# q loads cut by head, early loads gated behind weights, and v of batch 0 put ahead of the weights, in an attention and token/channel mixer kernel

## The chip, the cores and the metric

One core of a Trainium2 chip runs the whole program. The metric is device time in microseconds (us) of one launch; lower is better. The change is compared with the kernel before on the same inputs.

## What is computed

For 8 batches, 8 heads, 576 positions and head width 64, attention in which a position sees its neighbours within 32, and 8 global positions see and are seen by all; then a token mixer and a channel mixer on the 576 x 512 result.

```python
mask = (abs(pos[:, None] - pos[None, :]) <= 32) | is_global[:, None] | is_global[None, :]
attn = softmax(where(mask, q @ k.T / 8, -1e9))
x = attn @ v                                   # heads side by side: 576 x 512
u = x + (relu(x.T @ w_tok1) @ w_tok2).T        # w_tok1 576 x 256
out = u + relu(u @ w_ch1) @ w_ch2              # w_ch1 512 x 1536
```

Inputs and output are float32; the kernel computes in float16 with float32 sums.

## The kernel before, in words

Each engine runs its instructions in the order in which the program text issues them; nothing is reordered, so the text is the schedule. A batch goes through these stages: q and k are loaded as float32, cast to float16 (q on ACT, `cast_q`; k on POOL, `cast_k`), and transposed in 32 x 32 blocks on DVE (`Xk`, `Xq`). v is loaded in five pieces of 128 (the outer ones 96) rows, `load_v`, L94, and cast on POOL or ACT (`vcast`, L193). `S_step` makes the banded scores on PE and their exponentials on ACT (L259 to L265), `S_mask` multiplies by the band on DVE (L276), `GK` handles the global queries, `OG` (L304) the rows of the global positions, `PV` (L324 to L337) the product with v. `M1` to `M3` are the token mixer and a transpose, and `M4` (L411, weights wc1) and `M5` (L437, weights wc2) are the channel mixer, called dense here. `M4` and `M5` of batch b are merged, step by step, with the attention stages of batches b+1 and b+2. `fill(n)` issues n matmuls on zeros in the start.

The start (L560 to L717) is written out by hand for batch 0, and nothing dense lies beside it. SP issues all loads of q, v and later k, and all stores; POOL issues the loads that cast to float16 on the way (k of batch 0, w1, w2, wc1, wc2) and gathers q and k of the global positions (gq, gk). For batch 0, SP issues q for the two groups of four heads (hg = 0, 1), then v; POOL's weights stand ahead of its casts of v (L664 to L672, then L690). `load_qk(1)` and `load_v(1)` follow on SP. Later `load_wc2` stands on POOL ahead of the casts of v of batch 1 (L759, and `VC(1)` at L769).

Two points of order matter below. ACT casts both halves of q of batch 0 (L642) ahead of the first exponential, and all four casts of q of batch 1 (L136) ahead of the first ReLU of dense 0 (L414). And the builder gives SP's transfers eight completion semaphores in turn (DMAHW0 to DMAHW7 in the rows of the order; DMASW0 to 7 for POOL's): a transfer waits until the one eight before it has landed.

The load of q of one head group names the four heads as the outermost dimension of its source:

```python
nc.sync.dma_start(out=d[:, hg, 0 : 16 * D], in_=src[:, 0 : 4 * P].rearrange("h (i r) d -> h i (r d)", r=16))
```

Of the kernel before, what the change touches and what calls it, by code (L numbers as in the profile page):

```python
# [17 lines left out]
P = 128  # L18
# [13 lines left out]
def kernel(  # L32
# [79 lines left out]
    def load_q(b, hg):  # L112
        d = st[b]["q32"]
        src = q[b, 4 * hg : 4 * hg + 4]
        nc.sync.dma_start(out=d[:, hg, 0 : 16 * D], in_=src[:, 0 : 4 * P].rearrange("h (i r) d -> h i (r d)", r=16))
        nc.sync.dma_start(out=d[:, hg, 16 * D :], in_=src[:, 4 * P : S].rearrange("h (i r) d -> h i (r d)", r=2))

    def alloc_32(b):
# [4 lines left out]

    def load_qk(b):
        alloc_32(b)
        if b == 1:
            nc.gpsimd.memset(st[b]["k32"][:, :, RK * D - 2 : RK * D], 0.0)
        for hg in range(2):
            nc.sync.dma_start(
                out=st[b]["k32"][:, hg], in_=k[b, 4 * hg : 4 * hg + 4].rearrange("h (i r) d -> (h i) (r d)", i=32)  # L130
            )
            load_q(b, hg)
# [528 lines left out]

    nc.gpsimd.memset(n32v[0][0:WIN, 0], 0.0)
    nc.gpsimd.memset(n32v[0][P - WIN : P, NT - 1], 0.0)
    nc.gpsimd.dma_start(out=w1, in_=moe_w_tok1[0 : S - LAST, :].rearrange("(c p) x -> p c x", p=P))  # L664
    nc.gpsimd.dma_start(out=w1l[0:LAST, 0], in_=moe_w_tok1[S - LAST : S, :])
    nc.gpsimd.dma_start(out=w2[:, :, 0:S], in_=moe_w_tok2.rearrange("(c p) x -> p c x", p=P))

    def eg_const(i):
        for g in range(2):
            nc.gpsimd.tensor_copy(out=egs[i][:, :, :, g, NG:16], in_=ohk.unsqueeze(2).to_broadcast([P, NT, 4, NG]))  # L670

    load_wc1()  # L672
    eg_const(0)
    fill(FILL[1])
    u_S(0, 0, 0)()
    fill(FILL[2])
# [10 lines left out]
    )  # L687
    nc.vector.tensor_scalar(out=mf[:, 4 * QS :], in0=it_f[:, 4 * P : S], scalar1=gpp, scalar2=hi8, op0=ALU.is_equal, op1=ALU.max)
    globals_k(0, nc.vector)
    vcast(0, (0, 1, 2))  # L690
    load_qk(1)
    load_v(1)
    nc.gpsimd.memset(n32v[1][0:WIN, 0], 0.0)
    nc.gpsimd.memset(n32v[1][P - WIN : P, NT - 1], 0.0)
    make_identity(nc, ident)
# [2 lines left out]
    eg_const(1)  # L698
    globals_(1, nc.gpsimd)
    globals_k(1)  # L700
    u_S(0, 1, 1)()
    vcast(0, (3, 4), nc.scalar)
    fill(FILL[8])
# [51 lines left out]
    for hg in range(2):  # L755
        for half in range(2):
            cast_k(1, hg, half)
            cast_q(1, hg, half)
    load_wc2()  # L759
    nc.gpsimd.dma_start(out=w1l[LAST:P, 1], in_=moe_w_tok1[S - LAST : S, :])  # L760
    load_qk(2)
    load_v(2)
    for _, f in X_units(1):
        f()

    for b in range(B):
        D4, D5 = dense(b)
        if b == 0:
            merge(gap(2.5) + VC(1) + phase_s(1), D4)  # L769
            merge(gap(2.0) + weave(phase_og(1) + M1u(1), C(2)) + weave(phase_m(1), G(2) + X_units(2)), D5)  # L770
            flush()
            gather(gq, q, 1)
            gather(gk, k, 1)
        elif b == 1:
            merge(VC(2) + phase_s(2) + gap(1.0) + weave(phase_og(2) + M1u(2), C(3)), D4)
            for _, f in G(3) + X_units(3):
                f()
            gather_t(gq, gqT, 1)
            gather_t(gk, gkT, 1)
            merge(VC(3) + weave(mix(phase_m(2), phase_s(3))[:-2], C(4)) + mix(phase_m(2), phase_s(3))[-2:], D5)  # L780
            flush()
        else:
            A, Bs = [], []
            if b + 1 < B:
                A += phase_og(b + 1) + M1u(b + 1)
                Bs += phase_m(b + 1)
            if b + 2 < B:
                A = G(b + 2) + weave(A, X_units(b + 2) + VC(b + 2))
                Bs = mix(Bs, phase_s(b + 2))
            if b + 3 < B:  # L790
                Bs = weave(Bs[:-2], C(b + 3)) + Bs[-2:]
            merge(A, D4)
            merge(Bs, D5)
            flush()
# [30 lines left out]
```

## Time and profile before

| | |
|---|---|
| median of 3 runs | 369.27 us (368.64 to 370.51) |
| the profiled execution: its own time | 365.77 us |
| its span, first to last instruction | 364.1 us |
| mean granted TensorE clock | 0.958 |
| PE busy | 322.1 us (88%) |
| DVE, ACT, POOL busy | 188.8, 161.2, 74.5 us |
| data moved by DMA | 41.55 MB, mean 114 GB/s |

Times in the rows are microseconds from the start of the span. PE is the matrix engine, DVE the vector engine, ACT the activation engine, POOL the general engine, SP the engine that issues most transfers; SPq marks such an issue. A row of the timeline gives start, duration, engine, line, operation, out<-in with shapes, how many were merged (x), and in brackets how long the engine had stood idle and what released it. In a table of windows, the DMA share is the mean busy share of the core's 16 DMA engines: 0.25 is four of sixteen all the time. Transfers of several queues overlap on an engine, so it can be above 1. Bytes are counted where they land, so a float32 weight that is cast on the way counts half.

### The profile page before, as it was taken

What the parts mean: (1) busy time and instruction counts of PE and PEld (TensorE: products, weight loads), DVE (VectorE), ACT (ScalarE), POOL (GpSimd) and SP (SyncE); (2) the same over time, 40 slices, a digit from 0 to 9 for tenths busy, and PEclk for the clock granted to TensorE, in tenths of its full rate; (3) what the DMA queues carried; (4) which work ended last, traced back from release to release, by engine and by line L of the source; (5) the groups of instructions that cost most, each with busy time, mean ns of one, the idle gap of its engine ahead of it and who ended that gap; (6) DMA issues with size and microseconds to landing.
All of it is one profiled execution on the core that took longest, in us unless ns stands there. A gap on an engine that the chain in (4) does not pass through costs nothing.

```text
span 364.1 us, 7413 instructions
## 1 busy us (share of the span) xinstructions
PE 322.1 (88%) x3092; PEld 164.3 (45%) x3092; DVE 188.8 (52%) x355; ACT 161.2 (44%) x301; POOL 74.5 (20%) x155
## 2 busy tenths in 40 slices
PE   7239698798889996799989999999899999999994
PEld 2113453363436642354445644644466445545541
DVE  6257355464785753682659148745864466244021
ACT  5144128932295454242844546354645254411600
POOL 5711640326206001410141002300330000000000
PEclk9558899999899998999999999999999999999999
DMA  3996549847964937755164514511000021002012
GB/s 77 165 199 126 162 115 200 200 133 150 241 198 128 224 115 182 208 163 127 58 187 153 113 58 134 160 55 59 32 32 0 31 85 35 0 31 86 0 59 87
DMA packets 54738, 41.55 MB, mean 114 GB/s; under 512 B 39984, under 2 KB 46000, under 8 KB 54704
## 3 DMA queue, kind: packets, MB, share of 16 engines
q1 hardware_dynamic: 49136, 36.58, 36.3%
q0 software_dynamic: 5568, 4.49, 8.4%
q8 instruction: 24, 0.39, 0.5%
q14 instruction: 10, 0.08, 0.1%
HBM read 36.12 MB, written 9.44 MB: 125 GB/s over the span
## 4 chain that ended last, share of the span: by engine, by line
PE 53%; DMA 10%; ACT 6%; DVE 5%; SPq 2%; issue 2%; POOL 2%; POOLq 0%; DVEq 0%
PE b1p L411 17%; PE op L437 17%; DMA q<-in_q_dram 9%; DVE e_all L276 4%; PE hp L373 4%; PE a1p L357 3%; PE s L250 3%; PE b1lp L424 2%; ACT e_all L259 2%; PE pv L332 2%; PE pv L324 2%; PE pu L391 1%; PE pv L337 1%; SPq L94 1%; ACT e_all L265 1%
## 5 line engine op out<-in xcount | busy, mean ns | idle before, releaser
L437 PE MATMUL op<-wc,b 128*128 128x512 f16 x384 | 94.9, 380 | 0.0
L411 PE MATMUL b1p<-uT,wc 128*128 128x512 f16 x384 | 92.8, 383 | 0.9 <-ACT b L414 0.9
L414 ACT ACTIVATE b<-b1p 128x512 f16<-128x512 f32 x96 | 57.4, 601 | 65.6 <-PE b1p L411 65.3
L276 DVE TENSOR_TENSOR e_all<-e_all,bandm 128x1000 f16<-128x1000 f16 x64 | 40.1, 687 | 24.9 <-ACT e_all L265 24.8
L437 PEld LDWEIGHTS <-b 128*128 128x128 f16 x384 | 34.8, 98 | 38.8 <-issue 4.2
L411 PEld LDWEIGHTS <-wc 128*128 128x128 f16 x384 | 34.4, 98 | 38.8 <-issue 4.4
L441 DVE TENSOR_TENSOR osb<-u,op 128x512 f32<-128x512 f16 x32 | 22.0, 686 | 40.6 <-PE op L437 33.5
L259 ACT ACTIVATE e_all<-s 128x800 f16<-128x800 f32 x32 | 25.1, 837 | 39.8 <-PE s L250 39.5
L378 DVE TENSOR_TENSOR u<-x,hp 128x1024 f16<-128x1024 f16 x14 | 17.1, 1222 | 42.9 <-PE hp L373 42.9
L250 PE MATMUL s<-qT,kT 32*128 32x200 f16 (+1 forms) x640 | 23.1, 253 | 18.1 <-DVE qT L198 7.9
L279 POOL COPY eg<-e_all 128x160 f16<-128x160 f16 x14 | 5.2, 368 | 146.5 <-DVE e_all L276 146.5
L193 POOL CAST vsh<-v 128x512 f16<-128x512 f32 x38 | 23.4, 644 | 31.9 <-DMA v<-in_v_dram 31.9
L250 PEld LDWEIGHTS <-kT 32*128 32x128 f16 x640 | 13.3, 98 | 34.8 <-issue 27.9
L344 DVE TENSOR_TENSOR x<-pv,rr 128x512 f16<-128x512 f32 (+1 forms) x40 | 27.6, 691 | 1.4
L332 PE MATMUL pv<-vsh,e_all 128*128 128x66 f16 x320 | 28.1, 195 | 0.0
L332 PEld LDWEIGHTS <-e_all 128*128 128x128 f16 x320 | 24.3, 98 | 5.1 <-issue 0.5
L140 POOL CAST k<-k 128x576 f16<-128x576 f32 x28 | 17.8, 665 | 42.3 <-DVE kT L212 17.7
L136 ACT CAST q<-q 128x576 f16<-128x576 f32 x28 | 18.4, 681 | 15.6 <-DMA q<-in_q_dram 15.5
L102 PE MATMUL w<-zz 128*128 128x512 f16 x66 | 23.4, 475 | 1.3 <-DVE p_i L149 1.3
L337 PE MATMUL pv<-vsh,e_all 128*128 128x66 f16 x256 | 23.8, 195 | 0.0
L324 PE MATMUL pv<-rf,lf 128*128 128x264 f16 x80 | 22.0, 279 | 0.0
L212 DVE STREAM_TRANSPOSE kT<-k 128x576 int32<-128x576 int32 x16 | 19.9, 1242 | 3.7 <-DMA k<-in_k_dram 3.6
(134 smaller groups left out, 352.0 us busy)
## 6 DMA issues: line engine op xcount, KB each, us to landing
q<-in_q_dram SPq DMA_DIRECT2D x16, 512.0 KB
out_dram<-osb SPq DMA_DIRECT2D x32, 256.0 KB
k<-in_k_dram SPq DMA_DIRECT2D x14, 576.0 KB
v<-in_v_dram SPq DMA_DIRECT2D x24, 256.0 KB
v<-in_v_dram SPq DMA_DIRECT2D x16, 192.0 KB
wc<-in_moe_w_ch_dram POOLq DMA_DIRECT2D x6, 512.0 KB, 13.8
q<-in_q_dram SPq DMA_DIRECT2D x16, 64.0 KB
out_dram<-osb SPq DMA_DIRECT2D x8, 128.0 KB
```

The source lines that it names most:

```text
L102: nc.tensor.matmul(ps, lhsT=zz[:, 0:P], rhs=zz, start=True, stop=True)
L193: (nc.scalar.copy if eng else nc.gpsimd.tensor_copy)(out=vsh[b % 2][:, c, :, 0:D], in_=n32v[b % 2][:, c])
L250: nc.tensor.matmul(tiles[r // 2][:, r % 2, off : off + n], lhsT=kT[rs, P * c : P * c + P, e], rhs=qf[rs, lo : lo + n, e], start=(e == 0), ...
L259: nc.scalar.activation(out=e2[:, :, 1:3, 64:EW], in_=ps[:, :, 0:400].rearrange("p h (c x) -> p h c x", c=2), func=AF.Exp, scale=scale)
L276: nc.vector.tensor_mul(out=eh, in0=eh, in1=bandm)
L324: nc.tensor.matmul(ps[:, hf, 0 : 4 * VW], lhsT=lfs[b % 2][:, QS * tau - sh : QS * tau - sh + P], rhs=s["rf"][:, 4 * hf : 4 * hf + 4, :], s ...
L332: nc.tensor.matmul(o, lhsT=e_all[:, h, tau, QS - sh : QS - sh + P], rhs=vs[:, tau, h, :], start=False, stop=last and tau == NT - 1,)
L337: nc.tensor.matmul(o, lhsT=e_all[:, h, tau + 1, 0:P], rhs=vs[:, tau + 1, h, :], start=False, stop=last)
L344: nc.vector.tensor_tensor(out=x16[r, tau, :].rearrange("p (f h x) -> p f h x", f=2, h=4), in0=pq[r, :, :, 0:D], in1=rr[r].unsqueeze(3).to_ ...
L411: nc.tensor.matmul(ps, lhsT=wc1[:, cc, P * j : P * j + P], rhs=s["uT"][:, cc, :], start=(cc == 0), stop=(cc == 3))
L414: nc.scalar.activation(out=s["b1"][:, j, :], in_=ps, func=AF.Relu)
L437: nc.tensor.matmul(ps, lhsT=w, rhs=wc2[:, j, :], start=(j == 0), stop=(j == NJ - 1))
```

## The change

Four things. `load_q` issues four transfers of one head each (32 partitions x 1024) in place of one of four heads; the small rest (128 rows of 128) stays as it was. Ahead of the q and k loads of batches 1 and 2 stands a transfer of two float16 elements out of a weight tile into the k buffer: for batch 1 out of the second third of wc1, for batch 2 out of the second third of wc2. It can start only when that third has landed, and the load of k, which overwrites the same place, can start only after it. On POOL the weights of the start are moved behind the casts of v of batch 0 (w1 behind pieces 0 and 1, w2 and wc1 behind piece 2), and wc2 behind the casts of pieces 0 to 2 of v of batch 1; `load_qk(1)` and `load_v(1)` move down in the text. `VC(1)` is dissolved: its casts and `load_v(3)` stand ahead of dense 0.

```diff
--- before.py
+++ after.py
@@ -112,7 +112,11 @@
     def load_q(b, hg):
         d = st[b]["q32"]
         src = q[b, 4 * hg : 4 * hg + 4]
-        nc.sync.dma_start(out=d[:, hg, 0 : 16 * D], in_=src[:, 0 : 4 * P].rearrange("h (i r) d -> h i (r d)", r=16))
+        for r in range(4):
+            nc.sync.dma_start(
+                out=d[32 * r : 32 * r + 32, hg, 0 : 16 * D],
+                in_=src[r, 0 : 4 * P].rearrange("(i r) d -> i (r d)", r=16),
+            )
         nc.sync.dma_start(out=d[:, hg, 16 * D :], in_=src[:, 4 * P : S].rearrange("h (i r) d -> h i (r d)", r=2))
 
     def alloc_32(b):
@@ -123,8 +127,9 @@
 
     def load_qk(b):
         alloc_32(b)
-        if b == 1:
-            nc.gpsimd.memset(st[b]["k32"][:, :, RK * D - 2 : RK * D], 0.0)
+        if b in (1, 2):
+            src = wc1[0:1, 0, 512:514] if b == 1 else wc2[0:1, 4, 0:2]
+            nc.sync.dma_start(out=st[b]["k32"].bitcast(F16)[0:1, 0, 0:2], in_=src)
         for hg in range(2):
             nc.sync.dma_start(
                 out=st[b]["k32"][:, hg], in_=k[b, 4 * hg : 4 * hg + 4].rearrange("h (i r) d -> (h i) (r d)", i=32)
@@ -661,16 +666,18 @@
 
     nc.gpsimd.memset(n32v[0][0:WIN, 0], 0.0)
     nc.gpsimd.memset(n32v[0][P - WIN : P, NT - 1], 0.0)
-    nc.gpsimd.dma_start(out=w1, in_=moe_w_tok1[0 : S - LAST, :].rearrange("(c p) x -> p c x", p=P))
-    nc.gpsimd.dma_start(out=w1l[0:LAST, 0], in_=moe_w_tok1[S - LAST : S, :])
-    nc.gpsimd.dma_start(out=w2[:, :, 0:S], in_=moe_w_tok2.rearrange("(c p) x -> p c x", p=P))
 
     def eg_const(i):
         for g in range(2):
             nc.gpsimd.tensor_copy(out=egs[i][:, :, :, g, NG:16], in_=ohk.unsqueeze(2).to_broadcast([P, NT, 4, NG]))
 
+    eg_const(0)
+    vcast(0, (0, 1))
+    nc.gpsimd.dma_start(out=w1, in_=moe_w_tok1[0 : S - LAST, :].rearrange("(c p) x -> p c x", p=P))
+    nc.gpsimd.dma_start(out=w1l[0:LAST, 0], in_=moe_w_tok1[S - LAST : S, :])
+    vcast(0, (2,))
+    nc.gpsimd.dma_start(out=w2[:, :, 0:S], in_=moe_w_tok2.rearrange("(c p) x -> p c x", p=P))
     load_wc1()
-    eg_const(0)
     fill(FILL[1])
     u_S(0, 0, 0)()
     fill(FILL[2])
@@ -687,9 +694,6 @@
     )
     nc.vector.tensor_scalar(out=mf[:, 4 * QS :], in0=it_f[:, 4 * P : S], scalar1=gpp, scalar2=hi8, op0=ALU.is_equal, op1=ALU.max)
     globals_k(0, nc.vector)
-    vcast(0, (0, 1, 2))
-    load_qk(1)
-    load_v(1)
     nc.gpsimd.memset(n32v[1][0:WIN, 0], 0.0)
     nc.gpsimd.memset(n32v[1][P - WIN : P, NT - 1], 0.0)
     make_identity(nc, ident)
@@ -698,6 +702,8 @@
     eg_const(1)
     globals_(1, nc.gpsimd)
     globals_k(1)
+    load_qk(1)
+    load_v(1)
     u_S(0, 1, 1)()
     vcast(0, (3, 4), nc.scalar)
     fill(FILL[8])
@@ -756,17 +762,20 @@
         for half in range(2):
             cast_k(1, hg, half)
             cast_q(1, hg, half)
+    nc.gpsimd.dma_start(out=w1l[LAST:P, 1], in_=moe_w_tok1[S - LAST : S, :])
+    vcast(1, (0, 1, 2))
     load_wc2()
-    nc.gpsimd.dma_start(out=w1l[LAST:P, 1], in_=moe_w_tok1[S - LAST : S, :])
+    vcast(1, (3, 4))
     load_qk(2)
     load_v(2)
+    load_v(3)
     for _, f in X_units(1):
         f()
 
     for b in range(B):
         D4, D5 = dense(b)
         if b == 0:
-            merge(gap(2.5) + VC(1) + phase_s(1), D4)
+            merge(gap(2.5) + phase_s(1), D4)
             merge(gap(2.0) + weave(phase_og(1) + M1u(1), C(2)) + weave(phase_m(1), G(2) + X_units(2)), D5)
             flush()
             gather(gq, q, 1)
```

SP at the start of the program, before (q_0 and k_1: q of batch 0, k of batch 1):

```order
L84 DMA gidx_i<-in_global_idx_dram 128x16
L115 DMA q_0_118<-in_q_dram 128x1x1024
L116 DMA q_0_118<-in_q_dram 128x1x128
L115 DMA q_0_118<-in_q_dram 128x1x1024
L116 DMA q_0_118<-in_q_dram 128x1x128
L94 DMA v_0_85<-in_v_dram 96x8x64
L94 DMA v_0_85<-in_v_dram 128x8x64 x3
L94 DMA v_0_85<-in_v_dram 96x8x64
L129 DMA k_1_364<-in_k_dram 128x1152
```

And SP there in the changed kernel:

```order
L84 DMA gidx_i<-in_global_idx_dram 128x16
L116 DMA q_0_118<-in_q_dram 32x1024 x4
L120 DMA q_0_118<-in_q_dram 128x1x128
L116 DMA q_0_118<-in_q_dram 32x1024 x4
L120 DMA q_0_118<-in_q_dram 128x1x128
L94 DMA v_0_85<-in_v_dram 96x8x64
L94 DMA v_0_85<-in_v_dram 128x8x64 x3
L94 DMA v_0_85<-in_v_dram 96x8x64
L132 DMA k_1_384<-wc_107 1x2x1
L134 DMA k_1_384<-in_k_dram 128x1152
```

The order of q, v, k is the same; four rows of 32 partitions stand for each row of 128, and the gate (L132) has come ahead of k of batch 1. With the semaphores that each waits for, SP around the gate in the changed kernel reads:

```order
L94 DMA v_0_85<-in_v_dram 96x8x64 [waits DMAHW7_49]
L132 DMA k_1_384<-wc_107 1x2x1 [waits DMAHW0_49,DMASW2_49]
L134 DMA k_1_384<-in_k_dram 128x1152 [waits DMAHW1_49,DMAHW0_49]
L116 DMA q_1_383<-in_q_dram 32x1024 [waits DMAHW2_49,Activation_49]
L116 DMA q_1_383<-in_q_dram 32x1024 [waits DMAHW3_49]
```

DMASW2 is the semaphore of the second third of wc1, DMAHW0 then that of the gate. POOL from the gathers on, before (w_104, w_106: w1, w2; wc_107: wc1; vsh_100: v of batch 0 in float16):

```order
L183 DMA gk<-in_k_dram,idx_i 128x64 x2
L662 MEMSET v_0_85 32x512
L663 MEMSET v_0_85 32x512
L664 DMA w_104<-in_moe_w_tok_dram 128x4x256
L665 DMA w1l<-in_moe_w_tok_dram 64x256
L666 DMA w_106<-in_moe_w_tok_dram 128x2x576
L230 DMA wc_107<-in_moe_w_ch_dram 128x4x512 x3
L670 COPY eg_96<-ohk 128x20x8 x2
L193 CAST vsh_100<-v_0_85 128x8x64 x3
```

And POOL there in the changed kernel:

```order
L188 DMA gk<-in_k_dram,idx_i 128x64 x2
L667 MEMSET v_0_85 32x512
L668 MEMSET v_0_85 32x512
L672 COPY eg_96<-ohk 128x20x8 x2
L198 CAST vsh_100<-v_0_85 128x8x64 x2
L676 DMA w_104<-in_moe_w_tok_dram 128x4x256
L677 DMA w1l<-in_moe_w_tok_dram 64x256
L198 CAST vsh_100<-v_0_85 128x8x64
L679 DMA w_106<-in_moe_w_tok_dram 128x2x576
L235 DMA wc_107<-in_moe_w_ch_dram 128x4x512 x3
```

Each weight is now issued only after a cast that waits for a piece of v. On ACT, DVE and PE no instruction is added, removed or moved.

## Rows read from the trace of the kernel before

**Rows 1.** Table of windows, the start and the rest: us, engines, granted clock, DMA share, GB/s.

```profile
0.00:56.00 56.00, 36.10 (x319) 16.95 (x320) 27.93 (x89) 19.58 (x33) 25.00 (x54) 0.79 0.71 142
56.00:364.00 308.00, 286.05 (x2775) 147.33 (x2773) 160.89 (x267) 141.58 (x269) 49.50 (x101) 0.99 0.40 109
```

**Rows 2.** Timeline of SP, the first 40 us.

```profile
1.28 0.74 SPq L115 DMA_DIRECT2D q<-in_q_dram  x1
...
9.52 25.37 SPq L94 DMA_DIRECT2D v<-in_v_dram  x5
37.39 0.35 SPq L129 DMA_DIRECT2D k<-in_k_dram  x1
```

**Rows 3.** Timeline, all engines, the start: DVE, ACT, PE and POOL's waiting instructions.

```profile
8.56 1.26 DVE L212 STREAM_TRANSPOSE kT<-k 128x576 int32<-128x576 int32 x1 [1.36 <-DMA k<-in_k_dram]
...
13.32 1.15 ACT L642 CAST q<-q 128x1152 f16<-128x1152 f32 x1 [7.75 <-DMA q<-in_q_dram]
...
16.16 0.86 PE L250 MATMUL s<-qT,kT 32*128 32x200 f16 x16 [7.93 <-DVE qT L198]
...
18.48 1.26 DVE L212 STREAM_TRANSPOSE kT<-k 128x576 int32<-128x576 int32 x1 [2.29 <-DMA k<-in_k_dram]
...
22.49 1.15 ACT L642 CAST q<-q 128x1152 f16<-128x1152 f32 x1 [8.01 <-DMA q<-in_q_dram]
23.55 1.56 ACT L259 ACTIVATE e_all<-s 128x800 f16<-128x800 f32 x2
...
24.68 1.16 DVE L650 TENSOR_TENSOR bandm<-band,rowok 128x1000 f16<-128x1000 f16 x1
...
27.78 2.45 DVE L276 TENSOR_TENSOR e_all<-e_all,bandm 128x1000 f16<-128x1000 f16 x4
...
34.70 0.24 DVE L279 COPY eg<-e_all 128x160 f16<-128x160 f16 x1
...
36.70 0.61 POOL L193 CAST vsh<-v 128x512 f16<-128x512 f32 x1 [1.57 <-DMA v<-in_v_dram]
...
37.88 1.33 ACT L193 CAST vsh<-v 128x512 f16<-128x512 f32 x2 [4.72 <-POOL v L693]
...
39.93 0.63 PE L304 MATMUL og<-vsh,eg 128*32 128x132 f16 x20 [3.96 <-ACT lf L295]
...
55.75 2.40 ACT L136 CAST q<-q 128x576 f16<-128x576 f32 x4
...
55.93 1.89 PE L411 MATMUL b1p<-uT,wc 128*128 128x512 f16 x8
```

**Rows 4.** Table of windows of 2 us: columns as in rows 1.

```profile
24.00:26.00 2.00, 1.14 (x24) 0.68 (x23) 1.93 (x4) 1.10 (x2) 0.00 (x0) 0.50 1.22 197
...
122.00:124.00 2.00, 2.00 (x32) 1.74 (x30) 1.30 (x5) 1.85 (x4) 0.00 (x0) 1.00 1.14 288
...
128.00:130.00 2.00, 2.00 (x14) 0.75 (x16) 1.22 (x1) 0.00 (x0) 0.00 (x0) 1.00 0.25 100
```

**Rows 5.** Timeline of SP from 90 us: five pieces of v with little beside them.

```profile
89.76 5.71 SPq L94 DMA_DIRECT2D v<-in_v_dram  x5
```

**Rows 6.** The page's DMA issues: wc1 and wc2, KB landed each, us to landing.

```profile
wc<-in_moe_w_ch_dram POOLq DMA_DIRECT2D x6, 512.0 KB, 13.8
```

**Rows 7.** Table of windows 87:91, 93:99, 101:105, 138:142 and 148:152, its sum.

```profile
sum 22.00, PE 12.09 PEld 5.63 DVE 14.30 ACT 9.69 POOL 5.42; mean PE 2.42 PEld 1.13 DVE 2.86 ACT 1.94 POOL 1.08
```

**Rows 8.** Timeline: the first `M5`, the casts of q of batches 2 and 4, PE after the last.

```profile
73.82 2.11 PE L437 MATMUL op<-wc,b 128*128 128x512 f16 x9
...
87.17 1.36 ACT L136 CAST q<-q 128x576 f16<-128x576 f32 x2 [6.62 <-DMA q<-in_q_dram]
...
140.11 0.67 ACT L136 CAST q<-q 128x576 f16<-128x576 f32 x1 [4.11 <-DMA q<-in_q_dram]
...
141.57 0.61 PE L391 MATMUL pu<-ident,u 128*128 128x128 f16 x8 [3.31 <-ACT e_all L259]
```

**Rows 9.** Chain of waits, its part before 140 us: q of batch 4.

```profile
123.26 16.83 DMA q<-in_q_dram
```

## The prediction

> **What bounds the kernel now.** Start with the span of 364.1 us, cut in two by a table of windows [rows 1]. From 56 us on PE is busy 286 of 308 us at a granted clock of 0.99 (2.4 GHz nearly throughout): there it is the bound, and only its 22 us without work could be had. The first 56 us are another program: PE is busy 36 us, part of it on zeros, at a clock of 0.79, and dense work begins at 55.93 [rows 3]. So read the start first: who waits for what. ACT casts q of the first head group at 13.32 and of the second at 22.49, each after some 8 us idle, released by the DMA of q; the first exponential stands behind the second cast, at 23.55, though its scores were issued at 16.16. Then the global stage (OG) stands at 39.93, while its operand from the exponentials (eg) was ready at 34.94: the missing 5 us are v, whose third piece is cast at 36.70 and the last two at 37.88 [rows 3].
>
> Why are q and v so late? A table of short windows tells [rows 4]. From 128 to 130 us the DMA share is 0.25: four engines of sixteen, at 100 GB/s, and what is in flight then is q of batch 4 [rows 9]. SP's five issues of v take 25.4 us in the start [rows 2] and 5.7 us where little lies ahead of them [rows 5]. So v isn't slow in itself: it queues behind q on four engines and beside the weights. The same shows once more at 123 us: 16.8 us of DMA for q of batch 4 [rows 9], ACT idle 4.1 us for it, PE 3.3 us behind that [rows 8].
>
> **Part 1, the start.** (a) q on all engines. q of batch 0 and the first half of k land 1.18 + 0.29 MB. At 288 GB/s, reached from 122 to 124 us [rows 4], that is 5.1 us; with the issue at 1.28 [rows 2] and 2 us of latency, q is there at about 8 us. (The latency is an estimate: the last piece of v is issued by 9.52 + 25.37 = 34.89 and cast at 37.88, so 3 us is its upper end [rows 2, 3].) Ends: at once, or 22.5 as now. I take 8, because the mix in that row is the same (q and k). Casts then end by 10.4. The first k transpose stays at 8.56 (its issue isn't moved), the q transpose ends near 11. The scores also need the gathered global q, of which the rows show only that it was there by 16.16; I take 12.5 for the scores, and 13.4 for the first exponential, in place of 23.55.
>
> (b) From there to OG the engines' own work counts: exponentials, masks, eg; now eg ends 11.4 us after the first exponential (34.94 - 23.55). DVE has a second constraint, the second half of k, at 18.48 now. It is issued at about 9 and will meet v alone, not q and weights; I take 14; then come two transposes (1.26 us for k, as much for q), the band (from 24.68 to the first mask at 27.78 now, 3.1), two masks (2.45 each) and two eg copies (0.24 each): 25.0. By the exponentials eg ends at 13.4 + 11.4 = 24.8. I take 25.6 for what the two cost each other, and OG at 26.0: **13.9 us earlier** [rows 3]. Ends: with k unchanged at 18.48 DVE's sum gives 29.5 and OG 29.9 (10 us earlier), with scores at 11 and k at 12 OG stands near 24.4 (15.5 earlier).
>
> (c) v must not be later than that. SP reaches it at 9.5 as now (a POOL memset holds it, not moved); 5.7 us of pieces [rows 5] and 2 of latency give 17 to 18, some 20 beside k. ACT casts the last two behind the exponentials, that is one mask ahead of eg (about 23) and for 1.33 us [rows 3]: hidden. If this cover fails, each us later moves OG by one.
>
> (d) Weights behind v: w1 is issued at about 14.5, w2 and wc1 from 16. They land 2.15 MB; at the 197 GB/s of the mixed stretch at 24 us [rows 4], less what v takes of it, all of wc1 is there by 29 and its second third by about 27. A third takes 13.8 us to land now [rows 6], which from 17.5 would be 31.3. w1 is needed by the token mixer between OG (26) and dense 0, wc1 there, at 55.93 - 13.9 = 42: hidden.
>
> **Part 2, the gates.** Each adds one tiny transfer and a round trip on SP (2 us again, at most 3), and SP's later loads queue behind it; ACT waits for q. The first gate opens at about 27.3; q and k of batch 1 then flow from 29.5, 2.36 MB at 288 GB/s: 8.2 us, there by about 40. ACT's four casts of q stand ahead of dense 0, now at 55.75 [rows 3], then at 41.9. Hidden by 2 us; with wc1 at 31.3 it would be 1.6 us late. v of batch 1 lands to 46, wc2 goes out at about 44 to 47, its second third is there by 54, q of batch 2 by about 66. Dense 0 lasts 17.9 us to the first `M5` (73.82 - 55.93) [rows 3, 8], so that starts at 60. ACT is free for the second pair of casts of q of batch 2 at 80.55 now (87.17 - 6.62), 6.7 us behind the first `M5` [rows 8], so then at 66.7: hidden, just. The price of both gates is 0 on the path and up to 4 us if they slip.
>
> **Part 3, later batches.** Stalls of PE in five stretches around late q and what follows it sum to 22.0 - 12.1 = 9.9 us [rows 7]: ACT waiting for q of batch 2 (6.6 us idle at 87.17) and of batch 4 [rows 8], and masks behind the exponentials that come late for it. With 16 engines, q and k of a batch need 8 us, where the second half of q alone takes 16.8 now [rows 9], so the 3.3 us of PE and their sequel should go; the stalls that come from DVE's own order stay. I take half, **5 us**; ends 0 and 9.9. The six more issues on SP per batch (at most the 0.74 us of the first [rows 2], 4.4 us in the 308 / 8 = 38 of a batch) delay stores a little: 0, since three output buffers cover it; up to 2 us lost if not.
>
> Sum: 365.77 - 13.9 - 5 = 346.9 us on the profiled execution. The median of the runs shown stands 3.5 us above that execution; with the same distance I predict **350.5 us**.
>
> One rule of the Trainium skill speaks against this change, and the rest doesn't need it: "DMA: Bandwidth & Descriptors", section "Rules for kernel authors", says that transfers to disjoint partition ranges are no gain, as they serialize over the same engines, and that many small ones should be joined into a large one. By its formula (2 us and bytes at 436 GB/s per transfer, section "Anatomy of one DMA"), eight pieces one after another would take 18.4 us, and nothing would be won over the 16.8 of now. The trace disagrees as to pieces: five of v follow each other every 1.1 us [rows 5].
>
> **Rivals.** *Pieces serialize.* Eight transfers of 128 KB and two small ones land one after another and take as long as the two of now. Against it: pieces of v overlap [rows 5]. Then v still stands behind q, parts 1 and 3 vanish but for some 0 to 2 us from the weights' place: 367 to 370.
>
> *Given back at batch 1.* The start gains as computed, but the loads that the gates hold land 4 to 6 us after they are due, since weights, v and q together are limited by the same rate (197 GB/s at a share of 1.22 [rows 4]). Start 8 us, later 2: 355.8 + 3.5 = 359 us, 355 to 361. For it: my margin is 2 us. Against it: 288 GB/s was seen with q on a quarter of the engines.
>
> *Everything fits.* 15.5 + 9.9: 340.4 + 3.5 = 344 us.
>
> *The gates close the pipe, slower.* If v of batch 0 is slow by itself, its third piece is still cast at 36.7; then only are w2 and wc1 issued, the second third of wc1 lands 13.8 us later [rows 6] at about 51, the gate opens at 53, q of batch 1 comes at 63 to 72, and ACT holds dense 0 until then: 7 to 16 us later than 55.9, less at most 5 regained, so 2 to 11 lost to 365.8, plus 3.5: 371 to 381 us. From the third cast to q of batch 1 are at least 26 us (36.7 to 63), so it decides where that cast comes after about 30. Against it: 5.7 us for five pieces [rows 5]; for it: the 36.70 of now, and that I can't see v beside q on sixteen engines.
>
> **How the numbers follow.** Forecast (346 to 354) 0.56, given back 0.20, everything fits 0.12, serialize 0.06, slower 0.06. A measurement of this kernel tells about 0.5% (1.8 us) from no change. Faster is the first three, 0.88; same 0.06; slower 0.06. The range 343 to 361 holds the first three but for their outermost parts, about 0.85.
>
> **What would show it.** Right: no window of share 0.25 with only q in flight; the casts of q of batch 0 at about 8 and 9; first exponential at 13 to 14; v cast by 20; OG at 25 to 27, the first `M4` at 41 to 44; no ACT idle for q at batches 2 and 4. Wrong: casts of q of batch 1 that wait for DMA ahead of dense 0 (given back, or slower), v pieces still cast after 30, or an SP that stands at the gates while PE waits.

## The result, and the profile after

| | before | after |
|---|---|---|
| median of the runs side by side | 368.95 us (367.90 to 370.51) | 347.44 us (346.49 to 348.57) |
| ratio | 1 | 0.9415, 95% interval 0.9369 to 0.9461 |
| the profiled execution: its own time, span | 365.77, 364.1 us | 348.57, 346.8 us |
| mean granted TensorE clock | 0.958 | 0.973 |
| PE busy | 322.1 us (88%) | 319.5 us (92%) |

The kernel is faster by 5.85%. The prediction was 350.5 us, its range 343 to 361. But the experiments below say more than that number: one of the four parts of the change, used alone, gives 342.06 us, and the other three without it come out 1.4% slower than the kernel before.

Where did the time go? Read the same stretches as in [rows 1]. They are cut here at the first `M4` (40.19) and the first `M5` (64.17) of batch 0, the second of which was 73.82 before [rows 8], and at 133 us, just ahead of the first `M4` of batch 2 (151.60 before). The table of windows of the kernel after (columns as in [rows 1]):

```profile
0.00:40.00 40.00, 32.10 (x318) 15.27 (x319) 27.81 (x88) 19.29 (x32) 22.50 (x47) 0.91 0.96 181
40.00:64.00 24.00, 17.86 (x162) 7.19 (x161) 10.02 (x15) 16.16 (x33) 7.30 (x12) 0.86 0.90 166
64.00:133.00 69.00, 65.47 (x710) 34.56 (x708) 44.45 (x75) 33.99 (x67) 20.02 (x40) 0.98 0.93 203
133.00:346.80 213.80, 204.12 (x1907) 106.12 (x1906) 106.78 (x177) 91.56 (x171) 24.92 (x57) 1.00 0.29 77
```

And the kernel before, the stretches that answer to the second and the third:

```profile
56.00:74.00 18.00, 15.22 (x162) 6.57 (x161) 10.44 (x15) 15.79 (x32) 4.27 (x6) 1.00 1.01 201
74.00:151.00 77.00, 66.88 (x708) 34.63 (x706) 44.46 (x77) 34.23 (x66) 20.20 (x39) 0.96 0.69 178
```

The start is 16 us shorter (56 to 40), dense 0 is 6 us longer (18 to 24), the next stretch 8 us shorter (77 to 69), and from there on both kernels take 213 to 214 us. Within the third stretch PE does the same work (710 and 708 instructions), its idle time falls from 10.1 to 3.5 us, and its busy time by 1.4 us, at a granted clock of 0.98 in place of 0.96. Within the second it does the same 162 instructions, and idle time grows from 2.8 to 6.1 us, with 2.6 us more of busy time at a granted clock of 0.86.

SP's timeline after, to compare with [rows 2]:

```profile
9.54 5.41 SPq L94 DMA_DIRECT2D v<-in_v_dram  x5
29.70 0.68 SPq L132 DMA_DIRECT2D k<-wc  x1
31.38 0.35 SPq L134 DMA_DIRECT2D k<-in_k_dram  x1
...
58.46 0.65 SPq L132 DMA_DIRECT2D k<-wc  x1
60.41 0.35 SPq L134 DMA_DIRECT2D k<-in_k_dram  x1
```

The five issues of v take 5.41 us, not 25.37: nothing holds them any more. The gates are the two rows of L132. Each is followed by k some 1.7 to 2 us later: that is the round trip. Now rows picked from the timelines of all engines, in order of time, to compare with [rows 3] and [rows 8]:

```profile
8.98 1.15 ACT L647 CAST q<-q 128x1152 f16<-128x1152 f32 x1 [3.40 <-DMA q<-in_q_dram]
11.73 1.15 ACT L647 CAST q<-q 128x1152 f16<-128x1152 f32 x1 [1.60 <-DMA q<-in_q_dram]
12.57 0.86 PE L255 MATMUL s<-qT,kT 32*128 32x200 f16 x16 [4.33 <-DVE qT L203]
13.12 1.26 DVE L217 STREAM_TRANSPOSE kT<-k 128x576 int32<-128x576 int32 x1 [0.52 <-DMA k<-in_k_dram]
13.46 1.56 ACT L264 ACTIVATE e_all<-s 128x800 f16<-128x800 f32 x2 [0.57 <-PE s L255]
...
18.15 0.65 POOL L198 CAST vsh<-v 128x512 f16<-128x512 f32 x1
19.42 2.28 POOL L235 DMA_DIRECT2D wc<-in_moe_w_ch_dram  x3
...
24.73 0.24 DVE L284 COPY eg<-e_all 128x160 f16<-128x160 f16 x1
25.79 0.47 PE L309 MATMUL og<-vsh,eg 128*32 128x132 f16 x20
...
40.19 1.89 PE L416 MATMUL b1p<-uT,wc 128*128 128x512 f16 x8
44.41 1.36 ACT L141 CAST q<-q 128x576 f16<-128x576 f32 x2 [3.15 <-DMA q<-in_q_dram]
46.32 6.34 PE L416 MATMUL b1p<-uT,wc 128*128 128x512 f16 x16 [4.24 <-ACT b L419]
...
64.17 2.10 PE L442 MATMUL op<-wc,b 128*128 128x512 f16 x9
...
68.61 1.25 ACT L141 CAST q<-q 128x576 f16<-128x576 f32 x2 [3.64 <-DMA q<-in_q_dram]
74.48 1.24 ACT L141 CAST q<-q 128x576 f16<-128x576 f32 x2 [4.62 <-DMA q<-in_q_dram]
```

From the first exponential (13.46) to the `M4` (40.19) the rows stand 10 to 16 us earlier than in [rows 3], the third piece of v (18.15) some 18.5 us; what comes before the exponential is 3.6 to 10.8 us earlier. OG stands 0.8 us behind eg, with all of v cast, where it had to wait 5 us for v before. Then three rows show how part of it is given back. At 44.41 ACT casts the second half of q of batch 1, after 3.15 us idle for its DMA. The first ReLU of dense 0 stands behind that cast, so PE stands idle for 4.24 us behind its first 8 matmuls, from 42.08 on. When it resumes, 16 matmuls take 6.34 us. In a run below the same 16 take 3.61 us. The short windows of the kernel after show both the rate of the loads and the clock:

```profile
30.00:32.00 2.00, 2.00 (x34) 1.46 (x33) 1.84 (x6) 0.00 (x0) 0.00 (x0) 1.00 0.29 50
32.00:36.00 4.00, 3.91 (x19) 1.62 (x17) 1.14 (x2) 1.08 (x2) 0.04 (x1) 1.00 0.86 265
36.00:40.00 4.00, 3.87 (x31) 2.06 (x30) 2.15 (x4) 2.23 (x4) 1.24 (x2) 1.00 1.00 234
40.00:44.00 4.00, 2.08 (x10) 0.86 (x9) 3.54 (x5) 1.26 (x3) 1.76 (x3) 1.00 1.16 172
44.00:48.00 4.00, 1.68 (x5) 0.57 (x5) 1.58 (x3) 2.33 (x4) 1.23 (x2) 0.63 0.92 184
48.00:50.00 2.00, 2.00 (x6) 0.71 (x5) 0.00 (x0) 0.67 (x2) 1.72 (x3) 0.50 0.42 77
```

Behind the gate the DMA engines fall to a share of 0.29, and it is 0.48 in the first and 0.10 in the second of these two us: the gate waits for the second third of wc1, but little of the last third is then left to fill the gap. Then q and k of batch 1 flow at 265, 234 and 172 GB/s, slower from 36 us on and slowest beside v, which SP issues from 38.24 on. From 48 to 50 us the granted clock is 0.50 (1.2 GHz), after the 4.24 us that PE stood idle.

Two lines of the page of the kernel after stand against [rows 6] and [rows 9]: the weights land in 8.8 us, not 13.8, and no DMA of q is in the chain of waits that ended last.

```profile
wc<-in_moe_w_ch_dram POOLq DMA_DIRECT2D x6, 512.0 KB, 8.8
...
PE 70%; ACT 6%; DVE 5%; issue 2%; POOL 0%; POOLq 0%; DVEq 0%; ACTq 0%
```

### The profile page after: what moved, and what is told of

It is laid out like the page before. It is cut to its first block, busy times and chain, and to the rows that moved or that the text cites. A ratio compares the mean times of both kernels' runs of the same rounds, so it can differ in the third digit from the quotient of the medians.

```text
span 346.8 us, 7500 instructions
## 1 busy us (share of the span) xinstructions
PE 319.5 (92%) x3092; PEld 163.1 (47%) x3092; DVE 189.1 (55%) x355; ACT 161.0 (46%) x301; POOL 74.7 (22%) x154
## 4 chain that ended last, share of the span: by engine, by line
PE 70%; ACT 6%; DVE 5%; issue 2%; POOL 0%; POOLq 0%; DVEq 0%; ACTq 0%
PE op L442 23%; PE b1p L416 21%; PE hp L378 5%; PE a1p L362 4%; PE s L255 4%; DVE e_all L281 3%; PE b1lp L429 3%; PE pv L337 2%; PE pv L329 2%; ACT e_all L264 2%; PE pv L342 2%; PE pu L396 2%; ACT e_all L270 1%; ACT e_all L269 1%; PE og L309 1%
## 5 line engine op out<-in xcount | busy, mean ns | idle before, releaser
L416 PE MATMUL b1p<-uT,wc 128*128 128x512 f16 x384 | 95.1, 390 | 4.2 <-ACT b L419 4.2
L337 PE MATMUL pv<-vsh,e_all 128*128 128x66 f16 x320 | 27.6, 193 | 0.0
L342 PE MATMUL pv<-vsh,e_all 128*128 128x66 f16 x256 | 23.4, 193 | 0.0
L102 PE MATMUL w<-zz 128*128 128x512 f16 x66 | 21.1, 434 | 1.3 <-DVE p_i L154 1.3
```

The costliest lines, as they stand in the source:

```text
L337: nc.tensor.matmul(o, lhsT=e_all[:, h, tau, QS - sh : QS - sh + P], rhs=vs[:, tau, h, :], start=False, stop=last and tau == NT - 1,)
L342: nc.tensor.matmul(o, lhsT=e_all[:, h, tau + 1, 0:P], rhs=vs[:, tau + 1, h, :], start=False, stop=last)
L416: nc.tensor.matmul(ps, lhsT=wc1[:, cc, P * j : P * j + P], rhs=s["uT"][:, cc, :], start=(cc == 0), stop=(cc == 3))
```

## The experiments

The theory after the result: the cut of q gives the whole gain, and the order with the gates gives some of it back at batch 1. The rival: v ahead of the weights, and loads that do not collide, give a part of the gain. The runs went to several chips, so each is read by its ratio to runs of the kernel before on the same chip.

### The cut alone, and everything but the cut

First the kernel before, with only `load_q` taken from the change:

```diff
-        nc.sync.dma_start(out=d[:, hg, 0 : 16 * D], in_=src[:, 0 : 4 * P].rearrange("h (i r) d -> h i (r d)", r=16))
+        for r in range(4):
+            nc.sync.dma_start(out=d[32 * r : 32 * r + 32, hg, 0 : 16 * D], in_=src[r, 0 : 4 * P].rearrange("(i r) d -> i (r d)", r=16))
```

> The kernel before with the load of q cut by head and nothing else. My theory (q held four DMA engines and everything of SP queued behind it): the casts of q of batch 0 start near 9 and 12 us, the first exponential near 13.5, and v, though the weights now run beside it, is cast by 25, so OG stands at 26 to 28 and dense 0 begins at 41 to 43 instead of 55.9; in all 344 to 352 us, at least two thirds of the change's 21 us. Rival (the order of v and weights and the gates carry the gain): v stays behind the weights, its third piece is cast after 30, OG comes after 33, and the time is 357 to 366 us.

Measured: 342.06 us (341.78 to 343.03), ratio 0.9276 (0.9210 to 0.9343): better than either theory said. That interval lies wholly below the one of the full change. Rows of its timelines, SP, PE and ACT:

```profile
9.52 5.27 SPq L94 DMA_DIRECT2D v<-in_v_dram  x5
20.54 0.35 SPq L133 DMA_DIRECT2D k<-in_k_dram  x1
...
25.89 0.47 PE L308 MATMUL og<-vsh,eg 128*32 128x132 f16 x20
...
40.12 2.39 ACT L140 CAST q<-q 128x576 f16<-128x576 f32 x4
...
59.79 2.11 PE L441 MATMUL op<-wc,b 128*128 128x512 f16 x9
```

v is issued in 5.27 us although all weights stand ahead of its casts as before, POOL casts the first three pieces from 17.85 to 20.46, and OG stands at 25.89, against 25.79 in the full change. So the cut alone makes v early; the new order adds nothing there. And k of batch 1 is issued at 20.54, not 31.38, so its q is there when ACT comes to it at 40.12. The first `M5` is at 59.79, 4.4 us ahead of the full change. (ACT still waits 4.10 us for q of batch 2, at 65.89.)

Then the changed kernel with q in one transfer of four heads again (the diff above, the other way round):

> The changed kernel with q in one transfer of four heads again, order and gates kept. My theory: q of batch 0 needs 5.8 us per head group on four engines, so the casts start near 10 and 16 us, v queues behind q on these engines and is cast by 25 to 28, the weights wait for it, q of batch 1 comes after 50, and the stall at q of batch 4 is back: 358 to 370 us. Rival (order and gates carry the gain): 347 to 354 us.

Measured: 374.66 us (372.25 to 377.48), ratio 1.0141 (1.0058 to 1.0225): 1.4% slower than before, and slower than either theory said. Its timeline, ACT, and a window (columns as in [rows 1]):

```profile
23.63 1.15 ACT L643 CAST q<-q 128x1152 f16<-128x1152 f32 x1 [7.83 <-DMA q<-in_q_dram]
...
60.41 0.67 ACT L137 CAST q<-q 128x576 f16<-128x576 f32 x1 [7.00 <-DMA q<-in_q_dram]
```

```profile
52.00:56.00 4.00, 1.72 (x8) 0.68 (x7) 2.58 (x4) 1.34 (x2) 1.29 (x3) 1.00 0.26 98
```

q of batch 0 comes as late as in [rows 3]. OG is at 37.43, that is 2.5 us earlier than in [rows 3]: so much the order is worth in the start without the cut. But q of batch 1, held by the gate and again on four engines (share 0.26, 98 GB/s), makes ACT wait 7.00 us at 60.41, and the first `M5` comes at 79.64, 5.8 us later than in [rows 8].

### What sets the number of engines

If pieces as such brought the gain, two pieces should bring part of it. The changed kernel, order and gates kept, with q in two transfers of two heads:

```diff
-        for r in range(4):
-            nc.sync.dma_start(out=d[32 * r : 32 * r + 32, hg, 0 : 16 * D], in_=src[r, 0 : 4 * P].rearrange("(i r) d -> i (r d)", r=16))
+        for r in range(0, 4, 2):
+            nc.sync.dma_start(out=d[32 * r : 32 * r + 64, hg, 0 : 16 * D], in_=src[r : r + 2, 0 : 4 * P].rearrange("h (i r) d -> h i (r d)", r=16))
```

> The changed kernel with q in two transfers of two heads each (64 partitions) in place of four of one. If the outermost dimension of the source sets on how many engines a transfer runs, each of these runs on two engines, where the one of four heads ran on four: windows with q alone show a DMA share near 0.13 and some 50 GB/s, the casts of q of batch 0 start after 14 and 24 us, and the time is 385 to 440 us, slower than the kernel before. If what helped was smaller pieces, two pieces stand between one and four: 350 to 368 us.

Measured: 421.28 us (2 runs), ratio 1.1431 (1.1306 to 1.1556); the same kernel with one transfer of four heads had 1.0141, with four of one head 0.9415. A window in which q of batch 1 is in flight:

```profile
60.00:64.00 4.00, 1.43 (x7) 0.56 (x6) 1.38 (x2) 0.00 (x0) 0.00 (x0) 1.00 0.13 52
```

The share is 0.13 and the rate 52 GB/s: two of sixteen engines, where four heads outermost gave 0.25 and 100 GB/s [rows 4]. Two transfers of two heads do not share out over four engines: in the start two of them are issued by 2.55 us, and from 6 to 8 us the share is 0.14. So it is the size of the outermost dimension (2 heads, 4 heads, 32 rows) that sets the engines, and not the number of transfers. For the 32 rows this is read from the casts (8.98 and 11.73 us, against 13.32 and 22.49), since no row has q of one head alone in flight; and no run has one transfer of four heads with a large dimension outermost.

The small rest of q (128 rows of 128 floats) still has four heads outermost. The cut alone, with that rest cut by head as well:

```diff
-        nc.sync.dma_start(out=d[:, hg, 16 * D :], in_=src[:, 4 * P : S].rearrange("h (i r) d -> h i (r d)", r=2))
+        for r in range(4):
+            nc.sync.dma_start(out=d[32 * r : 32 * r + 32, hg, 16 * D :], in_=src[r, 4 * P : S].rearrange("(i r) d -> i (r d)", r=2))
```

> The kernel before with q cut by head, and the small rest of q (128 rows of 128 floats, four heads outermost) cut by head too. Theory A (the number of engines follows the outermost dimension for the rest also, but it is small and lies beside other loads): within 1 us of the cut alone, 341 to 342.5 us, first cast of q of batch 0 at 8.6 to 8.9 us. Theory B (the rest on four engines is what each cast of q now waits for): casts of q of batch 0 a microsecond earlier (8 and 10.5), start a microsecond shorter, 340.5 to 341.2 us.

Measured: 342.76 us (342.04 to 343.45), ratio 0.9299 (0.9257 to 0.9342): no difference that can be told from the cut alone. The first cast of q comes at 8.70, but the second only at 13.94, against 11.60 with the cut alone: sixteen issues stand on SP in place of ten, and the second group's take 3.05 us, not 1.89. OG slips to 27.35, and yet the first `M5` stands at 59.63. So 1.5 us at OG are not felt at the first `M5`.

### Weights, wc2 and the gates

Which of the three other parts gives the 5 us back? The changed kernel with w1, w2 and wc1 ahead of POOL's casts of v, as before:

```diff
     eg_const(0)
-    vcast(0, (0, 1))
     nc.gpsimd.dma_start(out=w1, in_=moe_w_tok1[0 : S - LAST, :].rearrange("(c p) x -> p c x", p=P))
     nc.gpsimd.dma_start(out=w1l[0:LAST, 0], in_=moe_w_tok1[S - LAST : S, :])
-    vcast(0, (2,))
     nc.gpsimd.dma_start(out=w2[:, :, 0:S], in_=moe_w_tok2.rearrange("(c p) x -> p c x", p=P))
     load_wc1()
+    vcast(0, (0, 1, 2))
```

> The changed kernel with w1, w2 and wc1 of the start ahead of POOL's casts of v again, q cut and gates kept. My theory (v was late behind q, not behind weights): v is 3 to 6 us later than in the changed kernel, which the exponentials mostly hide, and the weights land earlier, so the first gate opens 2 to 4 us earlier and the wait for q of batch 1 ahead of dense 0 (3.2 us of ACT, 4.2 of PE) shrinks: 343 to 350 us. Rival (v ahead of the weights is what brings the start forward): OG 5 us or more later, 352 to 360 us.

Measured: 343.95 us (343.40 to 344.14), ratio 0.9328 (0.9261 to 0.9396): some 3.5 us of the 5 are back. v is not 3 to 6 us late: POOL casts its first three pieces from 17.87 to 20.13, and OG is at 26.48. The gate opens 2.8 us earlier, and dense 0 hardly stops:

```profile
26.87 0.68 SPq L132 DMA_DIRECT2D k<-wc  x1
...
42.59 1.25 ACT L141 CAST q<-q 128x576 f16<-128x576 f32 x2 [0.64 <-DMA q<-in_q_dram]
44.38 3.61 PE L416 MATMUL b1p<-uT,wc 128*128 128x512 f16 x16 [1.60 <-ACT b L419]
```

ACT waits 0.64 us for q of batch 1, not 3.15; PE waits 1.60 us, and the 16 matmuls take 3.61 us, at the full clock.

The other way round, the weights left behind v and the two gate transfers taken out (`load_qk` then issues k and q as soon as SP comes to them):

```diff
-        if b in (1, 2):
-            src = wc1[0:1, 0, 512:514] if b == 1 else wc2[0:1, 4, 0:2]
-            nc.sync.dma_start(out=st[b]["k32"].bitcast(F16)[0:1, 0, 0:2], in_=src)
```

> The changed kernel without its two gate transfers. My theory (each gate costs a bubble of 2 us in the transfers and makes q of batch 1 come 3 us after it is due, after which PE runs 8 matmul groups at half clock): q of batch 1 is there before 38, dense 0 starts without the 4.2 us wait, its first M5 stands 4 to 7 us earlier: 340 to 344 us. Rival (the gates protect the weights and v from the loads of later batches): w1 or wc1 comes late, the token mixer or dense 0 waits for weights, 347 to 355 us.

Measured: 349.12 us (347.15 to 349.84), ratio 0.9453 (0.9376 to 0.9531). The first `M5` did come 4.3 us earlier (59.83), as the theory said, but the time lies in the range of the rival. Something else was late, a weight that the gates had protected, though not w1 or wc1. The table of waits of PE, first line (us in total, times, longest):

```profile
PE op L439 <- DMA wc<-in_moe_w_ch_dram: 5.0, 3, 2.4
```

PE waited three times for wc2, 5.0 us in all. wc2 is issued behind the casts of three pieces of v of batch 1, at 45.85 here, and then shares the engines with q and k of batch 2, which no gate holds any more. So the run that was to price the gates met the other half of the new order. The same kernel with wc2 put back ahead of those casts:

```diff
-    vcast(1, (0, 1, 2))
     load_wc2()
-    vcast(1, (3, 4))
+    vcast(1)
```

> The run without gates had the first M5 4.3 us earlier, as expected, but then PE waited 5.0 us for wc2, which POOL issues behind the casts of v of batch 1. Here the gates are gone and wc2 is issued ahead of these casts, as in the kernel before. If wc2's place took the gain back: no wait of M5 for wc2, 340 to 344 us. Rival: without gates the loads of batches 1 and 2 take the transfers from wc2 wherever it stands: M5 waits for wc2 again, 346 to 350 us.

Measured: 342.04 us (341.27 to 343.34), ratio 0.9269 (0.9192 to 0.9346), as expected, and no wait for wc2: 7.1 us less, of which the waits were 5.0. This kernel keeps the weights of the start behind v, and it equals the cut alone. So that order costs nothing by itself: it costs where a gate waits for those weights.

A gate that opens earlier, on the first third of wc1, in the full change:

```diff
-            src = wc1[0:1, 0, 512:514] if b == 1 else wc2[0:1, 4, 0:2]
+            src = wc1[0:1, 0, 0:2] if b == 1 else wc2[0:1, 4, 0:2]
```

> The changed kernel with the first gate on the first third of wc1 in place of the second. If the gate's lateness makes q of batch 1 late, the gate opens 2.5 to 4 us earlier (near 26 instead of 29.7), ACT waits less than 1 us for q of batch 1, PE does not fall to half clock, and the time is 341 to 344.5 us. Rival: q of batch 1 then shares the transfers with the last two thirds of wc1 and lands as late as before: 346 to 348.5 us.

Measured: 347.34 us (346.35 to 348.21), ratio 0.9422 (0.9341 to 0.9503): nothing gained.

```profile
27.96 0.68 SPq L132 DMA_DIRECT2D k<-wc  x1
30.73 0.35 SPq L134 DMA_DIRECT2D k<-in_k_dram  x1
...
44.37 1.24 ACT L141 CAST q<-q 128x576 f16<-128x576 f32 x2 [3.12 <-DMA q<-in_q_dram]
```

The gate opens 1.7 us earlier, k follows 0.65 us earlier, and the second half of q is cast at 44.37, against 44.41. So 1.1 of the 1.7 us go into the gate itself, whose round trip takes 2.77 us while the last thirds of wc1 still land, not 1.68. Why the other 0.65 us don't reach q is not shown; the rival's sharing with wc1 is one reading, v, which follows 0.8 us earlier on the same engines, another.

Last, the gates with all weights early and wc2 first (the edits of the runs on weights and on wc2 together), so that only the gates stand between it and the cut alone:

> The changed kernel with the weights of the start and wc2 back ahead of the casts of v, but with both gates: beside the run without gates and with wc2 first (342.04 us) and the one with the cut alone (342.06 us) it shows what the gates themselves cost. Theory A (each gate leaves the DMA engines empty for a round trip, but with the weights early the loads behind it land before they are due): no cost, 341.5 to 342.5 us, first M5 at 59.3 to 59.8 us. Theory B (the gates cost about a microsecond or two by themselves, as q of batch 1 or 2 or v of batch 1 comes late behind them): 343 to 345 us, with a wait of ACT for q of batch 1 or of PE for ACT b in dense 0.

Measured: 344.01 us (342.99 to 345.50), ratio 0.9330 (0.9286 to 0.9374); the two medians on this chip, 344.01 and 367.54 us, give 0.9360. Windows of this run:

```profile
54.00:56.00 2.00, 1.51 (x29) 0.78 (x27) 0.28 (x1) 1.79 (x5) 0.00 (x0) 1.00 0.53 113
56.00:58.00 2.00, 2.00 (x37) 0.83 (x35) 1.66 (x3) 2.00 (x6) 1.61 (x2) 1.00 0.07 15
...
84.00:88.00 4.00, 2.16 (x23) 0.92 (x22) 4.00 (x8) 2.70 (x8) 0.00 (x0) 0.78 1.03 224
88.00:92.00 4.00, 4.00 (x32) 1.32 (x30) 1.58 (x4) 3.50 (x8) 0.32 (x1) 0.50 1.03 227
```

The hole behind the second gate is plain (shares of 0.53 and 0.07; the gate is issued at 52.21, and k only at 57.20), and ACT waits 5.11 and 4.66 us for q of batch 2 behind it. But the first `M5` stands at 59.00 and the first `M4` of batch 1 at 81.73, no later than with the cut alone (59.79, 82.17). The profiled execution, the longest of the six, loses its 2.1 us after that, where PE idles from 84 to 88 us and then runs at a granted clock of 0.50. The same kernel without the second gate:

```diff
-        if b in (1, 2):
+        if b == 1:
```

> The run with both gates and the weights early, less the second gate. In that run the DMA share fell to 0.53 and 0.07 between 54 and 58 us behind the second gate, k of batch 2 was issued at 57.20, and q of batch 2 came late twice (5.11 and 4.66 us of ACT); the first M4 of batch 2 stood at 109.47, against 107.38 with the cut alone. Theory A (gate 2 alone cost those 2 us, gate 1 nothing): k of batch 2 issued before 52 us, no share under 0.5 between 50 and 64, M4 of batch 2 at 107 to 107.8, 341 to 342.5 us. Theory B (v of batch 1, which gate 1 holds back, makes SP late for q of batch 2 anyway): M4 of batch 2 at 109 or later, 343.5 to 344.5 us.

The row that this text calls the first `M4` of batch 2 is the first `M5` of batch 1; its numbers are those of that row. Measured: 343.19 us (341.96 to 344.98), ratio 0.9330 (0.9286 to 0.9374). A row of SP and a window:

```profile
45.45 4.54 SPq L134 DMA_DIRECT2D k<-in_k_dram  x1
```

```profile
88.00:92.00 4.00, 3.51 (x64) 1.60 (x64) 1.58 (x4) 3.86 (x11) 0.32 (x1) 1.00 0.84 222
```

k of batch 2 goes out 11.8 us earlier, the clock stays at 1.00, and the first `M5` of batch 1 is at 107.42, as the first theory had it; the time is 0.7 us above its range and below that of the second. The times of the two runs with gates and of the two without (342.04 and 342.06) lie within 2 us and their intervals overlap. So the price of the gates by themselves is some 0 to 2 us by the medians, and it stays open where in this interval.

The kernels with the cut, side by side:

| w1, w2, wc1 | wc2 | gates | us | ratio |
|---|---|---|---|---|
| ahead of v | ahead of v(1) | none | 342.06 | 0.9276 (0.9210 to 0.9343) |
| behind v | ahead of v(1) | none | 342.04 | 0.9269 (0.9192 to 0.9346) |
| ahead of v | ahead of v(1) | first | 343.19 | 0.9330 (0.9286 to 0.9374) |
| ahead of v | ahead of v(1) | both | 344.01 | 0.9330 (0.9286 to 0.9374) |
| ahead of v | behind v(1) | both | 343.95 | 0.9328 (0.9261 to 0.9396) |
| behind v | behind v(1) | both | 347.44 | 0.9415 (0.9369 to 0.9461) |
| behind v | behind v(1) | none | 349.12 | 0.9453 (0.9376 to 0.9531) |

By these medians late weights alone cost nothing and gates alone no more than 2 us; a late wc2 alone, with early weights and no gates, was not run. The losses appear in pairs: late weights with a gate that waits for them (3.5 us, with wc2 late in both kernels), and a late wc2 with no gate to hold the loads that it then meets (7.1 us, with the weights late in both).

### The half clock

Does the half clock in dense 0 cost what its rows say? The full change with 20 more matmuls on zeros ahead of dense 0, so that PE stands idle for less time behind its first eight:

> The changed kernel with 20 more matmuls on zeros ahead of dense 0, where PE stands 4.2 us and then runs at a granted clock of 0.5 for six more. The 20 last 4.3 us and delay the first M4 groups by no more than the wait. If the clock after the wait is a cost of its own, the six groups behind it run at 0.86 us each in place of 1.57 to 1.7, the first M5 stands 2.5 to 4 us earlier, and the time is 343 to 345.5 us. If only the wait for q costs, it stays at 346.5 to 348.5.

Measured: 346.28 us (345.56 to 346.75), ratio 0.9390 (0.9311 to 0.9468). Row and window:

```profile
46.92 3.61 PE L416 MATMUL b1p<-uT,wc 128*128 128x512 f16 x16 [0.47 <-ACT b L419]
```

```profile
44.00:48.00 4.00, 3.53 (x18) 1.47 (x17) 1.49 (x3) 2.35 (x5) 0.97 (x2) 1.00 1.14 187
```

The clock stays at 1.00, the 16 matmuls take 3.61 us in place of 6.34, and the first `M5` comes 2.1 us earlier, at 62.04: about half of the 4.4 us by which the full change is behind the cut alone there. The other half is left with the clock at 1.00 and goes with the late q. Of the 2.1 us, 1.2 are left in the median, just below the range of the second theory and above that of the first, and the intervals of the two ratios overlap; so the gain in the whole time is not told from none.

In the start PE also runs at 0.50 (10 to 16 us with the cut alone). On the kernel with all of q cut, 20 matmuls on zeros in place of 2 ahead of the first scores, and 3 in place of 7 behind the global queries:

```diff
-FILL = (14, 2, 4, 7, 4, 1, 4, 1, 9)
+FILL = (14, 20, 4, 3, 4, 1, 4, 1, 9)
```

> The kernel of the run before it (all of q cut by head, order of the kernel before), with 20 matmuls on zeros in place of 2 ahead of the first scores and 3 in place of 7 behind the global queries. Theory A (PE's clock falls to 0.50 about 10 us into the start because PE idles, and the start is paced by PE's scores and by a fill that stands ahead of OG): clock 1.00 through the first scores, OG near 25 us, 340 to 341.3 us. Theory B (the start is paced by ACT's exponentials and DVE's masks, and the clock there costs nothing): the same as the run before it within 0.5 us.

Measured: 342.63 us (341.65 to 344.46), ratio 0.9300 (0.9258 to 0.9342), as without it. A window of 4 us:

```profile
20.00:24.00 4.00, 4.00 (x33) 1.46 (x32) 3.75 (x10) 2.69 (x8) 3.70 (x11) 0.50 1.23 217
```

The number is that of the second theory, but the run doesn't settle it: the half clock was not taken away, it moved to 20 to 24 us, and OG stands at 27.68, against 27.35.

## Why the prediction was right, and where it was off

**Part 1, the start: right, OG to a few tenths, the gate not.** (a) The step "q on all engines" gave q at 8, scores at 12.5 and the first exponential at 13.4; they were at 8.98 (the cast), 12.57 and 13.46. The second cast came at 11.73, not at about 9; this cost nothing, as the scores waited for the gathered q until 12.57. (b) The second half of k was taken at 14 and came at 13.12; eg ended at 24.97 (25.6 taken), OG stood at 25.79 (26.0): 14.1 us earlier, 13.9 predicted. (c) v was cast at 18.15 (17 to 20 predicted). (d) The gate, that is the second third of wc1, opened at 29.70, where 27.3 was predicted: wc1 was issued from 19.42 on, behind the cast of the third piece of v at 18.15, where the text had w2 and wc1 go out from 16. The run with the cut alone shows that the gain of the start is the cut's, as the prediction's reading of [rows 2, 4] said; what it did not see is that (c) needs no new order either.

**Part 2, the gates: the failed step is the rate.** The text took 288 GB/s for q and k of batch 1, from a row in which q and k flowed [rows 4]. The rows after say 265, 234 and 172 GB/s, a mean of 224 from 32 to 44 us, with v behind them on the same engines. The gate was 2.4 us late as well, so that q was there at about 44.4, not 40, and ACT was due at about 41. The rival "given back" named this mechanism and 4 to 6 us for the lateness. What came was 3.15 us of waiting for q, then 4.24 us of idle PE, then the half clock: dense 0 took 24.0 us, not 17.9, so 6.1 us were given back against a stated 0 to 4. The half clock stands in no term of the prediction; PE's busy time in dense 0 grew by 2.6 us of the 6.1. One of its own signs of being wrong, casts of q of batch 1 that wait for DMA ahead of dense 0, came true. The price of both gates, taken as 0, is not theirs alone: with the weights early they cost 0 to 2 us. The 5.4 us between the full change and the cut alone (347.44 less 342.06) belong to the three other parts together, and with the weights and wc2 behind v the kernel without gates is no faster (349.12).

**Part 3, later batches: right in kind, too small.** Taken were 5 us of 0 to 9.9. The difference of the two spans is 17.3 us and the first `M5` is 9.65 us earlier, so 7.7 us came after it. ACT's waits for q of batch 4 are gone; those for q of batch 2 (3.64 and 4.62 us) remain, against the prediction's list of signs, but PE has only 3.5 us of idle time in the whole stretch. This part too is the cut's: from the first `M5` to the end of the span it is 290.3 us before, 282.6 after, 281.5 with the cut alone and 296.2 with everything but the cut.

**The sum, and how it fell near.** Predicted for the profiled execution were 18.9 us of gain, and 17.3 were measured: start 15.7 at the first `M4` (13.9 taken, as the matmuls between OG and dense 0 ran at a higher clock: 0.57 from 40 to 44 us before, 1.00 from 26 to 30 us after), dense 0 minus 6.1, later 7.7. Against the forecast that is 1.8 us more, 6.1 less and 2.7 more: that the sum is only 1.6 us off is luck, since the errors have opposite signs. The median came out 3.1 us lower than predicted, though the profiled execution was 1.7 us longer than predicted, since the profiled execution of before lay 3.2 us below its median and that of after 1.1 us above. The step "with the same distance" had no ground: it is scatter of one execution. (The sum there is 350.4, not 350.5.)

**The rule against pieces.** "DMA: Bandwidth & Descriptors" of the Trainium skill, section "Rules for kernel authors", says of two transfers to disjoint partition halves that they serialize over the same engines and that one transfer of 128 partitions should be used. Here the opposite is measured, 342.06 against 368.74 us on the same chip, because the one transfer has four heads outermost. The same section says that the slowest dimension that is not 1 confines a transfer to at most as many engines. With that rule the trace agrees: 52 GB/s for two heads, 100 GB/s for four [rows 4]. Joining does win where the pieces have fewer heads: one transfer of four heads against two of two, 1.0141 against 1.1431. No run here has both forms on all engines, so what joining is worth there is not shown. The formula of the Trainium skill, section "Anatomy of one DMA", from which the prediction took 18.4 us for eight pieces, is given there for transfers that POOL issues; q goes over SP's queue, and its eight pieces and two rests, issued from 1.27 us on, were cast at 8.98 and 11.73.

## What to carry to other kernels

Look for stretches where the DMA share stands at a small fraction (0.25, 0.13) while one load is in flight, and put a large dimension (here 32 rows in place of 4 heads) outermost in that load before anything is reordered: here one such edit gave all of the gain. A gate that holds loads back frees the engines for others, but what stands behind it must still land in time at the rate of the mixed stretch, not of the best one; and it ties its fate to whatever the gate waits for. After a change of several parts, run them apart: three of the four here were together worth less than nothing, 1.4% without the cut and 5.4 us with it.

## What the runs showed of the hardware that was not expected

Two transfers of two heads are far slower than one of four: in the changed kernel 421.28 against 374.66 us (1.1431 and 1.0141 of the kernel before on their chips), at 52 and 98 GB/s. Cutting in pieces can cost more than it can win. And transfers that use few engines hold up others on SP's queue: five issues of v took 25.37 us behind q of four heads [rows 2], 5.27 us behind q cut by head, with nothing else changed. It is the issues themselves that last, up to 7.82 us each before; SP's waits in that stretch name no transfer of q.
